# Moving weight splits one block ahead, a scaling behind the dealt work, and one product behind another, in an attention and two-layer expert kernel

## The chip, the cores and the metric

One Trainium2 chip, one of its cores. The metric is the device time of one execution in microseconds; the median of three runs of the kernel before is 670.41 us (670.06 to 671.7).

## What is computed

The reference chains three steps on 1152 tokens. Step 2 is where the change is.

```python
x = attention(q, k, v)                 # 8 heads, windowed or dilated, -> (1152, 512)
p = domain_probs / (domain_probs.sum(-1, keepdims=True) + 1e-09)
for e in range(4):                     # dense mixture: every token meets every expert
    h = np.maximum(x @ w1[e], 0.0)     # (1152, 512) @ (512, 1024)
    out += p[:, e:e + 1] * (h @ w2[e]) # (1152, 1024) @ (1024, 512)
h = out @ w_in                         # (1152, 512) @ (512, 2048)
g = P(h) / (Q(h) + 1e-6)               # a rational function, Q with |h|
return g @ w_out                       # (1152, 2048) @ (2048, 512)
```

## The kernel before

**Tiling.** Tokens lie in three chunks of 384 (c = 0, 1, 2), each of three tiles of 128 (t = 0 to 8). Hidden columns lie in units of 256 (u); two units are a group (g). Groups 0 to 7 are the four experts, groups 8 to 11 the last layer. Every fp32 operand is split into a high and a low part, and each product is made of three matmuls (high x high, high x low, low x high). The split of a weight is two steps: ScalarE casts the raw tile to its high part (line 777), VectorE subtracts it from the raw tile to get the low part (line 781), each in two halves of 128x512.

**A blocked group** (g = 2 to 7) has this order on TensorE (lines 994 to 1023). First `h_paced(u, 0)`, 24 matmuls of chunk 0 for the first unit (line 337); then the output tile 6 of the group before (`o_paced`, 12 matmuls, line 382); then `h_paced(u + 1, 0)` for the second unit; then output tiles 7 and 8. Behind these, `strassen(u, ...)` and `strassen(u + 1, ...)` make the hidden values of chunks 1 and 2 of one unit in seven products of six matmuls (line 886) in place of eight, with an output tile put between the products at three places (`then(0)`, `then(1)`, `then(2)`); the last tile of the second block is left out in group 7. In what follows a block is one call of `strassen`, a pair is two products in a row. In group 2 no output tile 6 stands ahead of the second unit.

**Inside a block.** The first product goes to `y`, and ScalarE copies it to `z` (line 900). Another product, the fifth, goes to `v`; ScalarE copies it to `p5` (line 904). The product that is third in the program, the sixth, is added up on `y`, and VectorE then adds `y` and `p5` into `v` (line 893). The next product on `y` has to wait for that sum, since it changes `y`.

**What sets the order.** A planner (`Pace`) deals the work of VectorE and ScalarE while it writes TensorE's program. `passed(us)` moves TensorE's planned clock on by the cost of a step (h 2.09 for half a chunk, o 2.74, p 1.045) and emits what VectorE can do by then. Two lists feed it. `later(wait, cost, key, f)` puts an item that is due at a set time. `behind(cost, key, f)` puts an item in a queue that is served in order; weight splits (`split_later`), sums of weight blocks (`sums_later`, line 797) and their casts (`sums_split_later`, lines 806 and 811) go there. What is left of VectorE's planned time is filled with pieces of the conversion of the last layer's float64 weights (`convert`, lines 140 to 182), whose result is stored through a single buffer `w` by SP's queue (line 145). `settle(key)` emits at once all that stands in the queue up to the named item; `h_paced(u, c)` settles the split of `w1[u]`.

**The output tile.** An output tile has one of two PSUM banks (`pso`). From group 1, tile 3 on until group 7, tile 0, ScalarE scales it by the expert's weight into `part` (line 412) and GpSimd adds `part` to the sum by a DMA (line 413). Elsewhere VectorE adds it (line 415).

**Raw weights.** They come by DMA into four buffers (line 84). The next three loads, `w1` of unit u + 3 and `w2` of units u + 2 and u + 3, are issued by SP once VectorE has made the low part of the sums of unit u + 1 (line 811).

Of the kernel before, what the change touches and what calls it, by code (L numbers as in the profile page):

```python
# [23 lines left out]
ALU = mybir.AluOpType  # L24
# [22 lines left out]
def body(ctx, tc, qkv, mask, dp, w1, w2, w1d, w2d, coef, out):  # L47
    nc = tc.nc
# [455 lines left out]
    with tc.manual_schedule():  # L504
# [353 lines left out]
        def o_paced(g, t):  # L858
            for v in range(2):
                settle(("h", 2 * g + v, t // 3))  # L860
                settle(("w2", 2 * g + v))
            ps = o_bank()
            for v in range(2):
                o_half(g, t, v, ps)
            if by_dma(g, t):
                o_sum(g, t, ps)
            passed(COST["o"])
            if not by_dma(g, t):
                later(0.2, COST["osum"], ("o", g, t), lambda: o_sum(g, t, ps))

        def strassen(u, between_):

            for k in (("w1", u), ("sw", u, 0), ("sw", u, 1), "tokens"):
                if k != ("sw", u, 0) or u % 2 == 0:
                    settle(k)
            yz, vz = h_tile(), h_tile()
            z, y, v, q = yz[:, 0, :TC], yz[:, 1, :TC], vz[:, 0, :TC], vz[:, 1, :TC]
            w = [i.rearrange("p (h k i f) -> p h i k f", h=2, k=2, i=2) for i in (w1s[u][:, 0], w1s[u][:, 1])]
            block = lambda m, h, i: [t[:, h, i] for t in m]
            x = lambda c, h: [t[:, 2 * h:2 * h + 2] for t in xt[c]]  # L880
            t_ = lambda n: [t[:, n] for t in tt]
            s = lambda h, i: [sw[u, i][:, n, h] for n in range(2)]
            def product(out, a, b, first=False):
                for k in range(2):
                    for n, (i, j) in enumerate(((0, 0), (0, 1), (1, 0))):
                        nc.tensor.matmul(  # L886
                            out, lhsT=a[i][:, k], rhs=b[j][:, k],
                            start=first and k + n == 0, stop=k + n == 3, skip_group_check=not first,
                        )
                passed(COST["p"])  # L890

            def add(out, a, b):
                later(0.2, COST["add"], ("add", u), lambda: nc.vector.tensor_tensor(out=out, in0=a, in1=b, op=ALU.add))

            def then(n):
                for f, *args in between_[n]:
                    f(*args)

            product(y, block(w, 0, 0), x(1, 0), first=True)
            nc.scalar.copy(z, y)  # L900
            then(0)
            product(v, s(1, 1), x(2, 0), first=True)
            p5 = st.tile([128, TC], F32, tag="p5", name="p5")
            nc.scalar.copy(p5, v)
            settle(("sw", u, 0))
            product(y, s(0, 0), t_(0))
            add(v, y, p5)
            then(1)
            settle(("add", u))
            product(y, s(0, 1), t_(1))  # L910
            add(q, y, p5)
            product(z, block(w, 1, 0), x(1, 1))
            then(2)
            settle(("add", u))
            product(v, s(1, 0), x(2, 1))
            product(y, block(w, 1, 1), t_(2))
            for c, ps, wait in ((1, yz, 1.1), (2, vz, 2.0)):
                high, low = relu_parts(u, c, ps)
                high()
                later(wait, COST["relu"], ("h", u, c), low)  # L920
# [42 lines left out]
        for g in range(NG):  # L963
            u = 2 * g
            more = g + 1 < NG
            again = g + 1 in BLOCKED
            o = lambda *at: [(o_paced, *i) for i in at]
            if g == 0:
                temp = token_sums()
                for v in range(2):  # L970
                    h_paced(v, 2)
                for j in range(3):
                    o_paced(0, 6 + j)
                continue
            if g == 1:
                loads((load_w2, u + 2), (load_w2, u + 3))
                split_later(w1s, "w1", u + 2)
                for n in range(3):
                    tokens_later(temp[n], *(t[:, n] for t in tt), wait=12.0)
                o_paced(1, 0)  # L980
                settle("tokens")
                t1 = first_sum()
                split_later(w2s, "w2", u + 2)
                split_later(w1s, "w1", u + 3)
                sums_later(u + 2)
                o_paced(1, 1)
                o_paced(1, 2)
                for v in range(2):
                    h_paced(u + v, 2)
                tokens_later(t1, *(t[:, :2] for t in xt[2]))  # L990
                sums_split_later(u + 2, 1)
                sums_split_later(u + 2, 0, [(loads, (load_w1, u + 4))])
                sums_later(u + 3)
                for j in range(3):
                    o_paced(1, 3 + j)
                continue
            if g in BLOCKED:
                h_paced(u, 0)
                sums_split_later(u + 1, 1)
                split_later(w2s, "w2", u + 1)  # L1000
                if again:
                    split_later(w1s, "w1", u + 2)
                if g > 2:
                    o_paced(g - 1, 6)
                h_paced(u + 1, 0)
                if g > 2:
                    o_paced(g - 1, 7)
                    o_paced(g - 1, 8)
                strassen(u, [o((g - 1, j if g > 2 else j + 3)) for j in (3, 4, 5)])
                sums_split_later(u + 1, 0, [(loads, (load_w1, u + 3), (load_w2, u + 2), (load_w2, u + 3))])  # L1010
                if again:
                    sums_later(u + 2)
                    sums_split_later(u + 2, 1)
                strassen(u + 1, (o((g, 0)), o((g, 1)), o((g, 2)) if again else []))
                if again:
                    sums_split_later(u + 2, 0, [(loads, (load_w1, u + 4))])
                    split_later(w2s, "w2", u + 2)
                    split_later(w1s, "w1", u + 3)
                    sums_later(u + 3)
                else:  # L1020
                    loads((load_w1, u + 4), (load_w1, u + 5))
                    o_paced(g, 2)
                    for j in range(3):
                        o_paced(g, 3 + j)
                        if j < 2:
                            settle(("o", g, 2))
                            x2_half(0, j)
                continue
            if g == NG1:
                while Pace.due:  # L1030
                    run_due(Pace.due.index(min(Pace.due)))
                st_pool.__exit__(None, None, None)
                Rational.pool = ctx.enter_context(tc.tile_pool(name="rat", bufs=3))
                o_tile(g - 1, 6)
                x2_half(1, 0)
                x2_half(1, 1)
                h_step(u, 0)
                h_step(u + 1, 0)
                between.clear()
                r1, r2 = pairs  # L1040
                r1.third()
                o_tile(g - 1, 7)
                r1.fourth()
                r1.fifth()
                o_tile(g - 1, 8)
                r2.denominator()
                r2.numerator()
            else:
                h_step(u, 0)
                h_step(u + 1, 0)  # L1050
                o_step(g - 1, 2)
            extra = {}
            if more:
                split_w1(u + 2)
                loads((load_w2, u + 2))
            h_step(u, 1)
            if g == NG1:
                x2_turn(2, 0)
                extra = {0: [(x2_turn, 2, 1), (x2_split, 2, 0), (x2_split, 2, 1)]}
            if more:  # L1060
                split_w1(u + 3)
                loads((load_w2, u + 3))
            h_step(u + 1, 1)
            if g == NG - 1:
                break
            o_step(g, 0, extra)
            if more:
                split_w2(u + 2)
            if g + 2 < NG:
                loads((load_w1, u + 4))  # L1070
            h_step(u, 2)
            if more:
                split_w2(u + 3)
            if g + 2 < NG:
                loads((load_w1, u + 5))
            h_step(u + 1, 2)
            o_step(g, 1)
# [150 lines left out]
```

## Time and profile before

| | |
|---|---|
| median of 3 runs | 670.41 us |
| the profiled execution | 670.22 us |
| its span, first to last instruction | 668.4 us |
| mean granted clock of TensorE | 0.988 of full speed |
| TensorE busy | 640.4 us, 96% of the span |
| VectorE busy | 501.6 us, 75% |
| ScalarE busy | 334.6 us, 50% |

The profiled execution lies 1.8 us over its span and 0.2 us under the median. TensorE is busy for nearly all of the span, and its busy time contains matmuls at half clock as well as at full clock. So what is to be had is read from two places: the time in which TensorE waits, and the stretches in which its granted clock is below full.

### The profile page before, as it was taken

Reading aid. Unit: us, or ns where it says so; the run is one execution under the profiler, and the core shown is the slowest. Engines: PE = TensorE matmul, PEld = TensorE weight load, DVE = VectorE, ACT = ScalarE, POOL = GpSimd, SP = SyncE. Lnnn points to the kernel's source line nnn. Section 1 sums busy time; section 2 is a strip of 40 time slices with the busy share of each in tenths; the row PEclk is TensorE's granted clock in tenths of the full one; section 3 lists DMA queues with packets and bytes.
Section 4 is the critical chain, followed back from the end, with each engine's and each line's share of the span. In section 5 each row is a group of like instructions: output and inputs, shape, how many; then the busy total and the mean of one; then the engine's idle time right before and its main releaser. Section 6 shows DMA issues by size and latency. Waiting matters only on the chain.

```text
span 668.4 us, 9664 instructions
## 1 busy us (share of the span) xinstructions
PE 640.4 (96%) x3766; PEld 567.6 (85%) x3767; DVE 501.6 (75%) x742; ACT 334.6 (50%) x621; POOL 83.0 (12%) x92
## 2 busy tenths in 40 slices
PE   8999999899989989989989989999999999999996
PEld 4888897798978878878978979889999999999985
DVE  6677249577766857876876874865899999999986
ACT  5986414244434444445444553324656555555551
POOL 2312080411102102111111111100000000000000
PEclk9999999999989989989999999999999999999999
DMA  9983024165936855864874883880330330300012
GB/s 283 256 232 117 1 64 151 71 151 135 264 111 158 255 139 141 238 204 102 249 199 112 256 239 76 241 336 1 126 119 9 126 126 1 126 0 1 1 48 94
DMA packets 33053, 92.92 MB, mean 139 GB/s; under 512 B 3536, under 2 KB 4048, under 8 KB 30960
## 3 DMA queue, kind: packets, MB, share of 16 engines
q1 hardware_dynamic: 25376, 78.77, 35.9%
q0 software_dynamic: 7344, 13.37, 11.5%
q8 instruction: 29, 0.48, 0.3%
q10 hardware_dynamic: 288, 0.16, 0.1%
q14 instruction: 16, 0.13, 0.1%
HBM read 59.79 MB, written 19.14 MB: 118 GB/s over the span
## 4 chain that ended last, share of the span: by engine, by line
PE 85%; DVE 8%; ACT 4%; issue 2%; DMA 1%; DVEq 0%; ACTq 0%
PE ps_o L382 39%; PE ps_h L337 29%; PE ps_h L886 12%; ACT pr L266 2%; PE ps_v L301 1%; PE ps_s L287 1%; DVE w L781 1%; DMA w<-w 1%; DVE hl L358 1%; DVE t L845 1%; PE ps_h L436 1%; PE ps_s L234 1%; DVE t L160 1%; ACT w L777 1%; PE ps_h L583 1%
## 5 line engine op out<-in xcount | busy, mean ns | idle before, releaser
L382 PE MATMUL ps_o<-w,hh 128*128 128x512 f32 x832 | 225.5, 393 | 2.1 <-DVE acc L415 2.1
L337 PE MATMUL ps_h<-xh,w 128*128 128x384 f32 x768 | 208.6, 345 | 13.6 <-ACT w L777 10.1
L382 PEld LDWEIGHTS ps_o<-w,hh 128*128 128x128 f32 x832 | 154.4, 188 | 32.4 <-DVE acc L415 2.8
L337 PEld LDWEIGHTS ps_h<-xh,w 128*128 128x128 f32 x768 | 142.8, 193 | 18.6 <-ACT w L777 12.2
L337 PE MATMUL ps_h<-xl,w 128*128 128x384 f32 x384 | 130.6, 340 | 0.0
L382 PE MATMUL ps_o<-w,hl 128*128 128x512 f32 x416 | 129.2, 392 | 0.9 <-DVE hl L358 0.9
L382 PEld LDWEIGHTS ps_o<-w,hl 128*128 128x128 f32 x416 | 77.8, 188 | 18.9 <-DVE hl L358 2.1
L412 ACT ACTIVATE part<-ps_o,p_sb 128x512 f32<-128x512 f32 x51 | 35.2, 690 | 105.1 <-PE ps_o L382 73.1
L358 DVE SCALAR_TENSOR_TENSOR hl<-ps_h,hh 128x768 fp32r<-128x768 f32 x48 | 44.7, 952 | 44.5 <-ACT hh L354 44.1
L413 POOL DMA_DIRECT2D acc<-part x51 | 44.5, 872 | 257.8 <-ACT part L412 241.9
L337 PEld LDWEIGHTS ps_h<-xl,w 128*128 128x128 f32 x384 | 74.1, 193 | 0.5
L354 ACT ACTIVATE hh<-ps_h 128x768 fp32r<-128x768 f32 x48 | 37.6, 809 | 58.1 <-PE ps_h L337 55.3
L474 ACT ACTIVATE ab<-sq,cbias 128x768 f32<-128x768 f32 x24 | 22.7, 944 | 37.2 <-DVE sq L470 36.9
L144 DVE TENSOR_TENSOR w<-f,w 128x512 fp32r<-128x512 f32 x32 | 22.0, 688 | 24.8 <-ACT w L140 24.7
L781 DVE TENSOR_TENSOR w<-raw,w 128x512 fp32r<-128x512 f32 x48 | 31.8, 685 | 8.5 <-ACT w L777 8.3
L465 ACT ACTIVATE sq<-ps_h 128x768 f32<-128x768 f32 x24 | 19.3, 803 | 32.3 <-PE ps_h L337 32.3
L140 ACT CAST w<-f 128x512 fp32r<-128x512 f32 x32 | 19.8, 619 | 26.7 <-DVE f L182 13.8
L266 ACT ACTIVATE pr<-pr,mx 128x80 f32<-128x80 f32 (+1 forms) x84 | 29.7, 357 | 6.6 <-DVE mx L259 6.5
L886 PE MATMUL ps_h<-xh,sw 128*128 128x384 f32 x96 | 29.1, 343 | 1.7 <-DVE hl L358 1.0
L886 PE MATMUL ps_h<-t,sw 128*128 128x384 f32 x144 | 29.6, 340 | 0.0
L886 PE MATMUL ps_h<-xh,w 128*128 128x384 f32 x96 | 28.3, 335 | 0.0
L777 ACT CAST w<-raw 128x512 fp32r<-128x512 f32 x48 | 28.1, 616 | 0.0
(94 smaller groups left out, 892.6 us busy)
## 6 DMA issues: line engine op xcount, KB each, us to landing
w<-w SPq DMA_DIRECT2D x32, 512.0 KB, 3.9
w<-w SPq DMA_DIRECT2D x16, 1024.0 KB, 6.8
raw<-in_w_dram SPq DMA_DIRECT2D x30, 512.0 KB, 6.4
acc<-part POOLq DMA_DIRECT2D x51, 256.0 KB, 4.2
x<-in_w1d_dram SPq DMA_DIRECT2D x16, 512.0 KB, 4.1
x<-in_w2d_dram SPq DMA_DIRECT2D x16, 512.0 KB, 3.7
out_dram<-acc SPq DMA_DIRECT2D x8, 256.0 KB, 2.2
v<-in_qkv_dram SPq DMA_DIRECT2D x6, 320.0 KB, 8.0
```

Of the source, the lines that this page charges most:

```text
L144: nc.vector.tensor_tensor(out=w[:, 1], in0=f, in1=w[:, 0].bitcast(F32), op=ALU.subtract)
L266: nc.scalar.activation(pr[:, j, i], pr[:, j, i], AF.Exp, scale=-1.0, bias=self.mx[:, j, i:i + 1], accum_out=self.total[:, j, i:i + 1],)
L337: nc.tensor.matmul(ps[:, i, :TC], lhsT=a[:, k, f], rhs=b[:, k], start=k + n == 0, stop=k + n == 5,)
L354: nc.scalar.activation(new_h(u, c)[0], ps[:, :, :TC], AF.Relu)
L358: nc.vector.scalar_tensor_tensor(out=hl, in0=ps[:, :, :TC], scalar=0.0, in1=hh.bitcast(F32), op0=ALU.max, op1=ALU.subtract,)
L382: nc.tensor.matmul(ps, lhsT=a[:, i, tk], rhs=b[:, i], start=v + n == 0, stop=v + n == 6)
L412: nc.scalar.activation(part, ps, AF.Copy, scale=pe)
L413: nc.gpsimd.dma_start(acc[t], part, accum_op=ALU.add)
L474: nc.scalar.activation(self.ab, self.sq, AF.Ln, bias=cbias)
L777: nc.scalar.copy(store[u][:, 0, s_], raws[nm, u][:, s_])
L781: nc.vector.tensor_tensor(out=w[:, 1, s_], in0=raws[nm, u][:, s_], in1=w[:, 0, s_].bitcast(F32), op=ALU.subtract)
L886: nc.tensor.matmul(out, lhsT=a[i][:, k], rhs=b[j][:, k], start=first and k + n == 0, stop=k + n == 3, skip_group_check=not first,)
```

## The change

Four edits, all in the groups of the experts.

- `o_paced`: the planner's time of the tile passes (and the work that is dealt for it is emitted) before ScalarE's scaling of the tile is emitted, not behind it.
- `strassen`: the sixth product goes ahead of the fifth. The sum of the two then follows ScalarE's copy of the fifth, and is due 0.8 us behind it, not 0.2 us behind the sixth.
- Blocked groups: the split of `w2[u + 2]` and `w1[u + 3]` is queued between the two blocks, not behind the second. The cast of the sums of unit u + 1, with the three loads that hang on it, is queued ahead of the last output tile of the first block, not behind the block.
- Group 1: the split of token sums is queued without its 12 us of delay, the split of `w1[u + 3]` follows it, and the second output tile goes ahead of the settling of the token sums.

```diff
@@ o_paced
             for v in range(2):
                 o_half(g, t, v, ps)
+            passed(COST["o"])
             if by_dma(g, t):
                 o_sum(g, t, ps)
-            passed(COST["o"])
-            if not by_dma(g, t):
+            else:
                 later(0.2, COST["osum"], ("o", g, t), lambda: o_sum(g, t, ps))
@@ strassen
             then(0)
+            settle(("sw", u, 0))
+            product(y, s(0, 0), t_(0))
             product(v, s(1, 1), x(2, 0), first=True)
             p5 = st.tile([128, TC], F32, tag="p5", name="p5")
             nc.scalar.copy(p5, v)
-            settle(("sw", u, 0))
-            product(y, s(0, 0), t_(0))
-            add(v, y, p5)
+            later(0.8, COST["add"], ("add", u), lambda: nc.vector.tensor_tensor(out=v, in0=y, in1=p5, op=ALU.add))
             then(1)
@@ group 1
                 for n in range(3):
-                    tokens_later(temp[n], *(t[:, n] for t in tt), wait=12.0)
+                    tokens_later(temp[n], *(t[:, n] for t in tt))
+                split_later(w1s, "w1", u + 3)
                 o_paced(1, 0)
+                o_paced(1, 1)
                 settle("tokens")
                 t1 = first_sum()
+                sums_later(u + 2)
                 split_later(w2s, "w2", u + 2)
-                split_later(w1s, "w1", u + 3)
-                sums_later(u + 2)
-                o_paced(1, 1)
                 o_paced(1, 2)
@@ blocked groups
-                strassen(u, [o((g - 1, j if g > 2 else j + 3)) for j in (3, 4, 5)])
-                sums_split_later(u + 1, 0, [(loads, (load_w1, u + 3), (load_w2, u + 2), (load_w2, u + 3))])
+                fills = [o((g - 1, j if g > 2 else j + 3)) for j in (3, 4, 5)]
+                free = [(loads, (load_w1, u + 3), (load_w2, u + 2), (load_w2, u + 3))]
+                fills[2].insert(0, (sums_split_later, u + 1, 0, free))
+                strassen(u, fills)
                 if again:
                     sums_later(u + 2)
                     sums_split_later(u + 2, 1)
+                    split_later(w2s, "w2", u + 2)
+                    split_later(w1s, "w1", u + 3)
                 strassen(u + 1, (o((g, 0)), o((g, 1)), o((g, 2)) if again else []))
                 if again:
                     sums_split_later(u + 2, 0, [(loads, (load_w1, u + 4))])
-                    split_later(w2s, "w2", u + 2)
-                    split_later(w1s, "w1", u + 3)
                     sums_later(u + 3)
```

The order of the instructions shows it at three places.

**Place 1: ScalarE at the start of group 4**, from the end of the block before to the relu (`hh`) of the second unit's chunk 0. `L777 CAST w1` is the high part of the second unit's weights, `L412` the scaling of output tile 6, `L140` and `L163` belong to the conversion. Before:

```order
L806 CAST sw_2479<-raw_2062 128x512
L777 CAST w2_2498<-raw_2358 128x512
L354 ACTIVATE hh_2500<-ps_h_2461 128x768
L412 ACTIVATE part_2516<-ps_o_2503,p_sb_82 128x512
L140 CAST w_2520<-f_2446 128x512
L163 ACTIVATE x64_2430<-x64_2430 128x512
L777 CAST w2_2498<-raw_2358 128x512
L777 CAST w1_2528<-raw_2356 128x512 x2
L354 ACTIVATE hh_2558<-ps_h_2533 128x768
```

and now, in the same stretch:

```order
L806 CAST sw_2500<-raw_2072 128x512
L354 ACTIVATE hh_2519<-ps_h_2485 128x768
L806 CAST sw_2540<-raw_2307 128x512
L412 ACTIVATE part_2542<-ps_o_2522,p_sb_82 128x512
L777 CAST w2_2564<-raw_2311 128x512
L140 CAST w_2578<-f_2470 128x512
L163 ACTIVATE x64_2426<-x64_2426 128x512
L777 CAST w2_2564<-raw_2311 128x512
L354 ACTIVATE hh_2587<-ps_h_2545 128x768
```

Both casts of the second unit's `w1` have left the stretch; they stood behind the scaling of tile 6 and ahead of the relu that ends it.

**Place 2: ScalarE in the block before that**, from the copy `z` (`L900`) to the end of the block; `L906` is the copy of the fifth product, `w1_2450` the weights that place 1 lost. Now:

```order
L900 COPY ps_h_2340<-ps_h_2340 128x384
L412 ACTIVATE part_2371<-ps_o_2355,p_sb_82 128x512
L806 CAST sw_2381<-raw_2072 128x512
L777 CAST w2_2394<-raw_2309 128x512
L906 COPY p5_2396<-ps_h_2341 128x384
L777 CAST w2_2394<-raw_2309 128x512
L412 ACTIVATE part_2415<-ps_o_2398,p_sb_82 128x512
L777 CAST w1_2450<-raw_2307 128x512
L140 CAST w_2453<-f_2385 128x512
L163 ACTIVATE x64_2324<-x64_2324 128x512
L777 CAST w1_2450<-raw_2307 128x512
L412 ACTIVATE part_2459<-ps_o_2436,p_sb_82 128x512
```

The first cast of `w2` for the next group now stands ahead of the copy of the fifth product, and it reads a tile whose load was issued in the block before.

**Place 3: VectorE in group 1**, around the low parts of the token sums (`L845`); `L415` adds an output tile and so frees its bank. Before:

```order
L409 TENSOR_SCALAR acc8_1473<-ps_o_1430,p_sb_82 128x512
L179 TENSOR_TENSOR f_1451<-f_1451,t_1428 128x512
L781 TENSOR_TENSOR w1_1471<-raw_849,w1_1471 128x512 x2
L845 TENSOR_TENSOR t1_1308<-ab_1306,t0_1307 128x768
L845 TENSOR_TENSOR t1_1308<-ab_1305,t0_1307 128x768
L845 TENSOR_TENSOR t1_1308<-ab_1304,t0_1307 128x768
L415 SCALAR_TENSOR_TENSOR acc0_864<-ps_o_1457,p_sb_82,acc0_864 128x512
```

and now:

```order
L409 TENSOR_SCALAR acc8_1473<-ps_o_1430,p_sb_82 128x512
L179 TENSOR_TENSOR f_1451<-f_1451,t_1428 128x512
L781 TENSOR_TENSOR w1_1471<-raw_849,w1_1471 128x512
L415 SCALAR_TENSOR_TENSOR acc0_864<-ps_o_1457,p_sb_82,acc0_864 128x512
L781 TENSOR_TENSOR w1_1471<-raw_849,w1_1471 128x512
L182 SCALAR_TENSOR_TENSOR f_1451<-x64_1350,f_1451 128x512
L845 TENSOR_TENSOR t1_1308<-ab_1306,t0_1307 128x768
```

The sum of group 1's first output tile has moved ahead of the three low parts.

## Rows read from the trace of the kernel before

**Rows 1.** The page: TensorE's granted clock in 40 slices, tenths of full speed.

```profile
PEclk9999999999989989989999999999999999999999
```

**Rows 2.** Waits of TensorE: total us, times, longest us.

```profile
PE ps_h L337 <- ACT w L777: 10.1, 5, 2.9
PE ps_o L382 <- DVE acc L415: 2.1, 1, 2.1
```

**Rows 3.** Timeline of ScalarE in group 4: start us, us.

```profile
241.56 0.69 ACT L412 ACTIVATE part<-ps_o,p_sb 128x512 f32<-128x512 f32 x1 [2.00 <-PE ps_o L382]
243.21 1.64 ACT L777 CAST w<-raw 128x512 fp32r<-128x512 f32 x3
```

**Rows 4.** Chain, five stalls: output tile 6, then tile 7 (start, us).

```profile
184.94 2.55 PE ps_o L382 x11
196.27 5.48 PE ps_o L382 x24
...
238.71 2.78 PE ps_o L382 x12
250.85 5.48 PE ps_o L382 x24
...
291.86 2.78 PE ps_o L382 x12
302.79 5.48 PE ps_o L382 x24
...
343.73 2.78 PE ps_o L382 x12
353.19 5.48 PE ps_o L382 x24
...
394.14 2.78 PE ps_o L382 x12
405.41 4.80 PE ps_o L382 x21
```

**Rows 5.** Chain, undisturbed: a pair, three products in a row, the same 24 matmuls.

```profile
260.16 2.10 PE ps_h L886 x12
269.89 3.14 PE ps_h L886 x18
287.70 4.16 PE ps_h L337 x24
```

**Rows 6.** Windows around the second and fourth stall: us, busy (x), PEclk, DMA, GB/s.

```profile
238.00:252.00 14.00, 10.90 (x47) 9.51 (x46) 6.16 (x11) 4.92 (x8) 0.89 (x1) 0.88 0.37 95
342.00:354.00 12.00, 10.00 (x51) 8.66 (x51) 6.69 (x10) 5.12 (x9) 0.86 (x1) 1.00 0.48 127
```

**Rows 7.** Chain, group 3's second block and group 7's end, where the tiles come late.

```profile
210.45 1.29 PE ps_h L886 x7
...
224.82 2.76 PE ps_o L382 x12
...
419.59 2.25 PE ps_h L886 x12
...
441.05 5.49 PE ps_o L382 x24
```

**Rows 8.** Timeline of ScalarE in group 3's second block.

```profile
221.37 0.62 ACT L140 CAST w<-f 128x512 fp32r<-128x512 f32 x1 [2.28 <-DMA w<-w]
222.97 0.48 ACT L900 COPY ps_h<-ps_h 128x384 f32<-128x384 f32 x1
```

**Rows 9.** The line of VectorE's sums in the blocks, ns min/median/max.

```profile
L893 DVE TENSOR_TENSOR ps_h<-ps_h,p x24: 555/566/567, 155.3 to 438.1; 128x384 f32<-128x384 f32 x24
```

**Rows 10.** The line of the raw loads, windows 220:232 and 324:336.

```profile
DMA to landing us min/median/max: 5.1/5.8/6.6
...
L84 SPq DMA_DIRECT2D raw<-in_w_dram x3: 328/616/1235, 324.4 to 328.1; - x3
DMA to landing us min/median/max: 6.5/7.5/8.2
```

## The prediction

> **What bounds the kernel now.** I read the page first: TensorE's granted clock is full except in a few slices [rows 1], so the question is where TensorE stands still and where the clock falls with it. The waits of TensorE come next. One cause holds most of them: five waits for ScalarE's cast of `w1`, 10.1 us together; a single wait of 2.1 us for a sum on VectorE is the next [rows 2].
>
> ScalarE's timeline shows why the cast is late. The settling of the second unit's weights puts the casts into ScalarE's program behind the scaling of output tile 6, and that scaling can only start when the tile is done, at 241.56. The casts follow from 243.21 on [rows 3]. But the end of tile 6 is just the moment at which TensorE wants the cast weights.
>
> The full price is more than the wait. The chain gives it as the time from the end of tile 6 to the start of tile 7, between which stand the second unit's 24 matmuls, 4.16 us when nothing disturbs them [rows 4, 5]:
>
> - 184.94 + 2.55 = 187.49 to 196.27: 8.78, lost 4.62
> - 241.49 to 250.85: 9.36, lost 5.20
> - 294.64 to 302.79: 8.15, lost 3.99
> - 346.51 to 353.19: 6.68, lost 2.52
> - 396.92 to 405.41: 8.49, lost 4.33
>
> Together 20.7 us. The part beyond the waits is the clock: around the second stall it is 0.88 on average over 14 us, so some 3.4 us at 1.2 GHz, half of which is lost; around the fourth, the shortest, it stays at 2.4 GHz [rows 6].
>
> **The change part by part.** The sum is made against the profiled execution, 670.2 us (span 668.4 and 1.8 around it), 0.2 under the median.
>
> *Splits one block ahead (with the scaling behind the dealt work).* The order shows both `w1` casts of the second unit in the block before (place 2), at two of its output tiles. One more block lies between them and their use: three tiles of 2.76 and seven products of about 1.05 are some 15 us, and the first unit's 24 matmuls and tile 6 come on top. So neither cast nor low part can be what TensorE waits for at the second unit. The moved work is four casts of ScalarE and four low parts of VectorE in each of five groups; no instruction is added. Inside the earlier block it lies beside TensorE's work: ScalarE is busy for half of the span. **-20.7 us**. The scaling's own move lets ScalarE use the time of a tile for the dealt casts instead of standing still until the tile is done; the two edits go together here.
>
> *Group 1.* The sum that frees the bank of the group's first tile now goes ahead of the three low parts of the token sums (place 3). The third tile needs that bank; it waited 2.1 us [rows 2]. **-2.1 us**. The second tile's sum is now behind the low parts, but its bank is wanted again only two h steps of 24 matmuls later, 8.3 us. Other work that the edit pulls forward (the split of `w1[u + 3]`) fills VectorE before its first use in group 2.
>
> *Fifth behind sixth, and what it gives the banks.* In the second block of group 3 the chain takes 14.37 us from 210.45 to the tile at 224.82 [rows 7]. A pair, a tile, three products, a tile and a pair are 2.10 + 2.76 + 3.14 + 2.76 + 2.10 = 12.86 [rows 5, 7], so 1.5 us are lost. There ScalarE held the relu and the copy behind a cast of the conversion that waited 2.28 us for the store of the single buffer [rows 8], and the fifth product, which starts on a PSUM tile, had to wait for that tile to come free. With the fifth behind the sixth it asks for the tile one product, 1.05 us, later. From 419.59 to 441.05, at the end of group 7, 21.46 us stand against three tiles, four pairs and three products in a row, 8.28 + 8.40 + 3.14 = 19.82, so 1.6 us. This stretch had conversion pieces in it; in the new order the last of them stand in group 7's first block. **-3.1 us**, both together, of which I would not be surprised to see a third stay.
>
> *What the swap takes.* The copy `z` had a product, a tile and nothing else to hide behind before the sixth product; it had the fifth in addition, and loses it: 2.76 us instead of 3.81. The sum of the two products had a tile less its own 0.56 us [rows 9] as slack; now the copy `p5` (as long as that of `z`, 0.48 us [rows 8]) comes first, so 1.7 us are left. I bound what may come of this from both sides. Below: nothing, if ScalarE is punctual. Above: two of twelve blocks as late as the copy at 222.97, 4.5 us behind the undisturbed end of its product at 218.45 [rows 8], so 4.5 + 0.5 - 2.76 = 2.2 us each. I take 0.7 us for all blocks, nearer to nothing, since the row's cause (a cast ahead of the copy that waits for a store) stands in the new order at two second blocks only, with some 7 us between the stores there.
>
> *Loads one block closer to their use.* In four groups the first `w2` cast now stands ahead of the copy `p5` (place 2). Count from the end of the product behind the second tile in the block before (line 910), which is the last to read the buffer that the sums of the next unit go to. ScalarE casts the sums, VectorE makes the low part behind about four of its own items: an estimate of 3.1 us from casts of about 0.55 [rows 3] and sums of 0.56 [rows 9]. SP then issues `w1`, and `w2` up to 1.2 us later; a load of these trios lands 5.1 to 8.2 us behind its issue [rows 10]. That is 8.2 to 12.5. Up to the cast, TensorE makes four products and two tiles, 4.2 + 5.5 = 9.7, and ScalarE a scaling and a cast, so it is there at about 11.0. The product that wants the sum of this block comes behind two more products and a tile: 6 x 1.05 + 3 x 2.76 = 14.6. The cast, the copy and the sum take some 1.7 us. So a load may land at 12.9 before TensorE notices, 0.4 us behind the slowest one. Bounds: 0, and 2 us in each of four groups if landing is as much later as the trios vary (3.1 us). I take 0.7 us in all. [...]
>
> Sum: 20.7 + 2.1 + 3.1 = 25.9 off, 1.4 on: 670.2 - 24.5 = **645.7 us**.
>
> **The rivals.**
>
> *The loads come late (B).* With the new casts of `w2` ahead of the copy `p5`, ScalarE waits for DMA and TensorE with it. For it: the margin is 0.4 us, and VectorE, with the same work in 25 us less, may run behind. Against: the first landings of the trios are well inside. Four waits of 2 us give 645.7 + 8 = 654; if they pull the clock down as the second stall did, four of 4.5, some 663.
>
> *The conversion holds ScalarE (C).* Its casts, dealt during a tile, wait for the store of the single buffer and now stand ahead of a scaling or a copy. Two or three waits of 2.2 us: about 651.
>
> *Every block waits for `z` (D), the slower side.* ScalarE's copy stands behind the scaling, which itself stands behind the dealt casts, and the sixth product asks for it 1.05 us sooner. If that were as late in every block as in [rows 8], twelve waits of 2.2 us eat 26 us: 671, and with the clock's fall, some 2 us each by the stalls above, about 695. It decides from 2.1 us per block on. Against: the dealt casts now run during the tile, so the scaling's queue gets shorter, not longer.
>
> *Nothing moves (E).* The second unit's wait stays because something else ends it then (the raw load). Against: its load is issued a whole block earlier than its cast. About 669.
>
> **How the numbers follow.** My forecast, new waits of 0 to 3.5 us, has 0.74: 644 to 648. B 0.12, C 0.09, D 0.03, E 0.02. The range takes in the forecast, C, and B's lower half, and below it half a microsecond more of small waits that may go: 643.5 to 652.5. A measurement of this kernel can tell about 0.3%, 2.0 us, from no change; faster by more than that has 0.95, same 0.02, slower 0.03.
>
> **What would show it.** In the profile of the changed kernel the row of TensorE waiting for the cast of `w1` is gone; tile 6 to tile 7 takes 4.2 us in every group; the granted clock has no slice below full between 100 and 440 us; group 1's third tile follows the second at once. A wait of TensorE for the copy or the sum in the blocks, or of ScalarE's cast on a raw load, would show B or C, and in all twelve blocks D. I am wrong if the five stalls stay, or if waits inside the blocks sum to over 5 us.

## The result, and the profile after

The changed kernel takes 646.22 us (median of 4 runs, 645.87 to 646.3) against 670.23 of the kernel before beside it: a ratio of 0.964, 95% interval 0.962 to 0.966. The forecast was 645.7. Its profiled execution took 646.3 us.

The page of the profiled execution: its span, the busy engines, TensorE's granted clock in 40 slices, and the engines' shares of the chain of waits.

```profile
span 644.5 us, 9658 instructions
...
PE 630.6 (98%) x3767; PEld 562.4 (87%) x3767; DVE 502.0 (78%) x742; ACT 334.7 (52%) x621; POOL 83.0 (13%) x92
...
PEclk9999999999999999999999999999999999999999
...
PE 92%; DVE 5%; ACT 2%; issue 0%; DVEq 0%; ACTq 0%
```

TensorE is busy for 630.6 us in place of 640.4, with the same matmuls: what is less is the time of matmuls that ran at half clock in the slices of [rows 1]. VectorE and ScalarE do the work that they did before. The waits of TensorE (total, times, longest):

```profile
PE ps_h L337 <- DVE hl L358: 2.0, 1, 2.0
...
PE ps_o L382 <- DVE hl L358: 0.9, 1, 0.9
PE ps_h L886 <- DVE ps_h L893: 0.7, 1, 0.7
```

Both rows of [rows 2] are gone. The 2.0 lies in the attention at 35 us and the 0.9 in front of group 1, at 107; the 0.7 is the only one of this table in the blocked groups. The chain (start us, us) has, in order of time, group 1's tiles, the five places of [rows 4] (the first with tile 6, the second unit's 24 matmuls, and tiles 7 and 8; of the others the 24 matmuls), and the two places in the blocks where something is left:

```profile
107.63 14.37 PE ps_o L382 x62
122.00 8.35 PE ps_h L337 x48
...
182.33 2.76 PE ps_o L382 x12
185.09 4.18 PE ps_h L337 x24
189.28 5.48 PE ps_o L382 x24
...
232.99 4.18 PE ps_h L337 x24
...
251.34 0.04 issue
251.39 2.38 PE ps_h L886 x12
...
281.19 4.18 PE ps_h L337 x24
...
329.08 4.18 PE ps_h L337 x24
...
376.98 4.18 PE ps_h L337 x24
...
395.34 2.10 PE ps_h L886 x12
...
410.98 2.12 PE ps_h L886 x12
...
413.12 0.57 DVE ps_h L893
...
413.74 2.37 PE ps_h L886 x12
416.12 5.49 PE ps_o L382 x24
```

The second unit takes 4.18 us in every group (4.16 in [rows 5]). The two places left are a pair that starts late in group 4's first block (2.38 + 0.04 for 2.10, 0.3 us), and the end of group 7, where two pairs take 416.12 - 410.98 = 5.14 in place of 4.20. The late pair in the timelines of ScalarE and VectorE: the conversion's cast waits for the store of its buffer, and the copy `p5` and the sum stand behind it.

```profile
249.17 0.62 ACT L140 CAST w<-f 128x512 fp32r<-128x512 f32 x1 [1.91 <-DMA w<-w]
...
250.77 0.57 DVE L907 TENSOR_TENSOR ps_h<-ps_h,p 128x384 f32<-128x384 f32 x1 [0.25 <-ACT p L906]
```

The tiles at the end of group 7 begin at 416.12, in [rows 7] at 441.05: 24.93 us earlier. Piece by piece: the five stretches of [rows 4] give 41.46 - 5 x 4.18 = 20.6; group 1's tiles end at 122.00, in the chain of before at 124.38, 2.4; group 3's stretch of [rows 7] takes 12.88, 1.5; the end of group 7 gives 0.7 (20.78 from 395.34 to 416.12, where [rows 7] have 21.46); group 4's late pair takes 0.3. Together 24.9.

At the last output tiles it is still 24.97 (613.26, before 638.23), but the spans differ by 23.9 only. From the end of VectorE's last sum to the end of the span, where the profile shows no engine at work any more, the changed kernel takes 5.1 us (639.42 to 644.5) and the kernel before 4.0 (664.42 to 668.4). Of the twelve traces below, two (`after_again`, `minus_scaling`) have 5.1 as well and ten have 4.0 to 4.2. Taking back the splits, the swap, the early loads or group 1's order by itself ends it, so it is no one edit's price. So where kernels differ by about 1 us, the medians are set beside a stretch of the traces that does not contain this end: from the start of group 1's tiles to the start of the last output tiles, 107.63 to 613.26, 505.6 us in the changed kernel.

### The profile page after: what moved, and what is told of

It is laid out like the page before. It is cut to its first block, busy times and chain, and to the rows that moved or that the text cites. A ratio compares the mean times of both kernels' runs of the same rounds, so it can differ in the third digit from the quotient of the medians.

```text
span 644.5 us, 9658 instructions
## 1 busy us (share of the span) xinstructions
PE 630.6 (98%) x3767; PEld 562.4 (87%) x3767; DVE 502.0 (78%) x742; ACT 334.7 (52%) x621; POOL 83.0 (13%) x92
## 4 chain that ended last, share of the span: by engine, by line
PE 92%; DVE 5%; ACT 2%; issue 0%; DVEq 0%; ACTq 0%
PE ps_o L382 43%; PE ps_h L337 30%; PE ps_h L886 14%; PE ps_v L301 2%; PE ps_s L287 1%; PE ps_s L234 1%; ACT pr L266 1%; PE ps_h L436 1%; PE ps_h L583 1%; PE ps_h L382 0%; DVE t L160 0%; DVE hl L358 0%; ACT pt L291 0%; DVE u L480 0%; DVE acc L421 0%
## 5 line engine op out<-in xcount | busy, mean ns | idle before, releaser
L337 PE MATMUL ps_h<-xh,w 128*128 128x384 f32 x768 | 202.9, 337 | 2.0 <-DVE hl L358 2.0
L337 PEld LDWEIGHTS ps_h<-xh,w 128*128 128x128 f32 x768 | 139.3, 188 | 3.4 <-DVE hl L358 2.2
L337 PE MATMUL ps_h<-xl,w 128*128 128x384 f32 x384 | 128.5, 335 | 0.0
L337 PEld LDWEIGHTS ps_h<-xl,w 128*128 128x128 f32 x384 | 72.1, 188 | 0.7
L412 ACT ACTIVATE part<-ps_o,p_sb 128x512 f32<-128x512 f32 x51 | 35.1, 688 | 68.3 <-PE ps_o L382 43.4
L358 DVE SCALAR_TENSOR_TENSOR hl<-ps_h,hh 128x768 fp32r<-128x768 f32 x48 | 44.7, 952 | 27.8 <-ACT hh L354 27.6
L140 ACT CAST w<-f 128x512 fp32r<-128x512 f32 x32 | 19.8, 618 | 20.1 <-DMA w<-w 11.2
L777 ACT CAST w<-raw 128x512 fp32r<-128x512 f32 x48 | 28.5, 615 | 1.1 <-DMA raw<-in_w_dram 1.1
L163 ACT ACTIVATE x<-x 128x512 f32<-128x512 f32 x32 | 21.7, 679 | 13.3 <-DVE t L160 13.2
```

The source lines that it names most:

```text
L337: nc.tensor.matmul(ps[:, i, :TC], lhsT=a[:, k, f], rhs=b[:, k], start=k + n == 0, stop=k + n == 5,)
L358: nc.vector.scalar_tensor_tensor(out=hl, in0=ps[:, :, :TC], scalar=0.0, in1=hh.bitcast(F32), op0=ALU.max, op1=ALU.subtract,)
L412: nc.scalar.activation(part, ps, AF.Copy, scale=pe)
L777: nc.scalar.copy(store[u][:, 0, s_], raws[nm, u][:, s_])
```

## The experiments

Twelve runs were made, ten kernels and two repeats, in three comparisons of four, each beside the kernel before: 671.43, 670.71 and 670.49 us. What was to be told apart is which edit carries the gain. My theory was the forecast's: the splits' place is the gain, the scaling only goes with it, the swap of fifth and sixth cures the late blocks. The rival was that ScalarE's scaling is the point, since all that stands behind it waits for a tile.

### One edit alone

`only_scaling` is the kernel before with the first edit:

```diff
+            passed(COST["o"])
             if by_dma(g, t):
                 o_sum(g, t, ps)
-            passed(COST["o"])
-            if not by_dma(g, t):
+            else:
```

> The kernel before with one edit: ScalarE's scaling of an output tile behind the work dealt for that time. My theory (the casts of the second unit's w1 are emitted by the settling at the second unit, behind tile 6 as a whole): the five stalls stay, shorter by the one or two casts that now precede the scaling; 1 to 4 us faster than before, 666 to 669 us, TensorE still waits five times for the cast of w1, over 7 us in total. Rival (the scaling's place is what held the casts): the stalls go, 650 to 653 us.

664.58 us (664.23 to 666.58), ratio 0.9913, interval 0.9881 to 0.9946. It gives more than mine said and far less than the rival's. Its waits of TensorE, and two of the five stalls as windows (us, busy and count of PE, PEld, DVE, ACT, POOL, then PEclk, DMA share, GB/s):

```profile
PE ps_h L337 <- ACT w L777: 9.1, 5, 1.9
```

```profile
236.00:250.00 14.00, 12.01 (x58) 10.13 (x58) 7.61 (x14) 5.95 (x10) 0.89 (x1) 1.00 0.30 85
288.00:302.00 14.00, 11.96 (x51) 10.24 (x50) 6.37 (x12) 4.12 (x7) 0.87 (x1) 0.88 0.33 95
```

The five stalls stay, but the longest is 1.9 us, not 2.9, and at three of them the clock holds at 2.4 GHz. From tile 6 to tile 7 it is 6.7, 6.7, 8.2, 6.7 and 8.2 us: 15.6 lost, not 20.7. The shorter waits and the clock are 5.1 us of gain. Three more places differ: group 3's stretch of [rows 7] is undisturbed (12.88), the end of group 7 takes 20.78 in place of 21.46, and group 1's tiles take 1.6 more, with the clock down. Together that makes 5.7 us; the spans (668.4 and 662.8) differ by 5.6. What the scaling leaves standing are the five waits.

`only_splits` is the kernel before with the edit of the blocked groups alone (the fourth hunk of the change).

> The kernel before with one edit: the blocked groups' queue (splits between the two blocks, sums and loads ahead of the first block's last tile). My theory: this alone takes the five stalls, 20.7 us, whatever the scaling's place: 648 to 651 us, no wait of TensorE for the cast of w1, the 2.1 us of group 1 and some of the late banks stay. Rival (the dealt casts now stand behind scalings in the blocks, ScalarE comes late to the copies, so both edits are needed): 655 to 662 us with waits of TensorE for ScalarE's copies or VectorE's sums inside the blocks.

653.83 us (653.64 to 653.93), ratio 0.9746, interval 0.9712 to 0.978: between the two. The waits of TensorE:

```profile
PE ps_h L886 <- DVE ps_h L893: 2.5, 4, 0.8
...
PE ps_h L886 <- DVE hl L358: 1.0, 4, 0.3
```

The five stalls are gone, but new short waits for VectorE stand in the blocks, and group 1's wait of 2.1 us stays.

### One edit taken back

In `minus_splits` both splits of `w2[u + 2]` and `w1[u + 3]` are queued behind the second block again; the rest is the changed kernel.

```diff
-                    split_later(w2s, "w2", u + 2)
-                    split_later(w1s, "w1", u + 3)
                 strassen(u + 1, (o((g, 0)), o((g, 1)), o((g, 2)) if again else []))
                 if again:
                     sums_split_later(u + 2, 0, [(loads, (load_w1, u + 4))])
+                    split_later(w2s, "w2", u + 2)
+                    split_later(w1s, "w1", u + 3)
```

> The changed kernel with the split of w2[u + 2] and w1[u + 3] queued behind the second block again; scaling, swap, loads and group 1 stay as changed. If the splits' place is what took the five stalls: they come back as in the run with the scaling's edit alone (TensorE waits five times for the cast of w1, 9 to 10 us, and loses 14 to 17 us in all), 660 to 663 us. If the scaling's place took most of them: 650 us or less.

666.35 us (665.27 to 668.29), ratio 0.9935, interval 0.9915 to 0.9956. The five waits are back as in `only_scaling`, and the end of group 7 is worse than in any other kernel here:

```profile
PE ps_h L337 <- ACT w L777: 9.1, 5, 1.9
PE ps_h L886 <- DVE ps_h L893: 3.8, 1, 3.8
```

So the place of the splits is worth 20 us within the change. In this trace it is 8.3, 8.0, 6.7, 8.2 and 6.7 us from tile 6 to tile 7, so 17.1 lost, with the clock down at three places; another 4.7 are lost at the end of group 7, where it is 23.40 us from the first block's last tile to the tiles at the end, and 18.68 in the changed kernel. Together 21.8; the profiled execution took 667.69 us, 21.4 more than that of the changed kernel. In the chain, with the DMA of the conversion's single buffer in it (415.13 and 438.53 begin and end the 23.40):

```profile
415.13 2.42 PE ps_o L382 x11
...
423.74 8.25 DMA w<-w
...
434.62 3.91 PE ps_h L886 x12
438.53 5.46 PE ps_o L382 x24
```

The last pair takes 3.91 us in place of 2.1: the granted clock is down as well, 0.83 on average from 430 to 440 us.

`minus_scaling` is the changed kernel without the first edit.

```diff
-            passed(COST["o"])
             if by_dma(g, t):
                 o_sum(g, t, ps)
-            else:
+            passed(COST["o"])
+            if not by_dma(g, t):
```

> The changed kernel with the scaling ahead of the dealt work again. My theory: the scaling's place only uses slack of ScalarE: 646 to 648 us, within 1.5 us of the changed kernel. Rival (the two edits work together): 650 to 658 us, with waits inside the blocks.

652.84 us (651.69 to 653.25), ratio 0.9729, interval 0.9699 to 0.976. My theory fell here: within the change the scaling's edit carries 6.6 us (6.1 in the stretch from group 1's tiles to the last output tiles), although no stall at the second unit came back. TensorE waits inside the blocks:

```profile
PE ps_h L886 <- DVE ps_h L907: 4.0, 4, 1.5
```

(Line 907 is the first sum, `y` and `p5`; L893 is the others.) Group 3's first block shows how. Timelines of this kernel: ScalarE, VectorE, TensorE (start us, us, what, idle before and what ended it).

```profile
195.00 0.69 ACT L412 ACTIVATE part<-ps_o,p_sb 128x512 f32<-128x512 f32 x1 [2.03 <-PE ps_o L382]
195.58 0.61 ACT L777 CAST w<-raw 128x512 fp32r<-128x512 f32 x1
...
197.69 0.48 ACT L900 COPY ps_h<-ps_h 128x384 f32<-128x384 f32 x1
...
196.74 0.69 DVE L144 TENSOR_TENSOR w<-f,w 128x512 fp32r<-128x512 f32 x1 [4.02 <-ACT w L140]
...
204.53 0.56 DVE L907 TENSOR_TENSOR ps_h<-ps_h,p 128x384 f32<-128x384 f32 x1
...
205.14 1.33 PE L886 MATMUL ps_h<-t,sw 128*128 128x384 f32 x6 [1.54 <-DVE ps_h L907]
```

and the same stretch of the changed kernel:

```profile
192.71 0.61 ACT L777 CAST w<-raw 128x512 fp32r<-128x512 f32 x1
...
194.84 0.69 ACT L412 ACTIVATE part<-ps_o,p_sb 128x512 f32<-128x512 f32 x1
195.86 0.46 ACT L900 COPY ps_h<-ps_h 128x384 f32<-128x384 f32 x1 [0.32 <-PE ps_h L886]
...
193.87 0.69 DVE L144 TENSOR_TENSOR w<-f,w 128x512 fp32r<-128x512 f32 x1 [1.55 <-ACT w L140]
...
202.42 0.56 DVE L907 TENSOR_TENSOR ps_h<-ps_h,p 128x384 f32<-128x384 f32 x1
...
203.29 1.23 PE L886 MATMUL ps_h<-t,sw 128*128 128x384 f32 x6
```

With the scaling ahead, ScalarE stands still until the tile is done at 195, and the weight cast follows 2.9 us later than in the changed kernel. Behind it stands a cast of the conversion (L140). VectorE, which makes the low parts of these casts in its own order, stands still for that one for 4.02 us (1.55 in the changed kernel) and comes 2.1 us later to the sum, and TensorE stands still for the sum, 1.5 us. Group 5 has the same picture. In groups 4 and 6 TensorE waits 0.45 us, and there the sum also waits for the copy `p5`, which stands behind a conversion cast that waits for the store of its buffer.

Between 160 and 430 us VectorE waits for the weight casts 16.8 us (first row: this kernel) and 1.7 us in the changed kernel (second row); with the casts of the sums and of the conversion it is 43.8 against 19.8. ScalarE waits for output tiles 72.0 (third row) against 39.9 us, with nearly the same busy time in that window, 128.8 and 128.4:

```profile
DVE w L781 <- ACT w L777: 16.8, 9, 3.0
...
DVE w L781 <- ACT w L777: 1.7, 3, 1.1
...
ACT part L412 <- PE ps_o L382: 72.0, 35, 5.0
```

`minus_swap` is the changed kernel with the fifth product ahead of the sixth and the sum due 0.2 us behind the sixth, as before.

```diff
-            settle(("sw", u, 0))
-            product(y, s(0, 0), t_(0))
             product(v, s(1, 1), x(2, 0), first=True)
...
+            settle(("sw", u, 0))
+            product(y, s(0, 0), t_(0))
+            add(v, y, p5)
             then(1)
```

> The changed kernel with the fifth product ahead of the sixth again. My theory: the swap gives the fifth product's PSUM tile 1.05 us more, worth 0 to 2 us where the relu before it is late: 646 to 648.5 us. Rival (the swap's cost, the later copy of the fifth product ahead of the sum, shows): 645.5 us or less, without the 0.3 us that TensorE now loses behind the second tile in group 4's first block.

644.98 us (644.52 to 645.77), ratio 0.9616, interval 0.9587 to 0.9645. The late block of group 3 does not come back: its chain has nothing but pairs and tiles of the usual length. So the swap is not needed for it; `only_scaling`, with the old order of the products, has it undisturbed too. A second comparison, below, asks for the swap's price.

`late_loads` puts the cast of the sums and the loads that hang on it behind the first block again; the splits stay early.

```diff
-                fills[2].insert(0, (sums_split_later, u + 1, 0, free))
                 strassen(u, fills)
+                sums_split_later(u + 1, 0, free)
```

> The changed kernel with the cast of the sums of unit u + 1, and the three raw loads that hang on it, queued behind the first block again, 4 to 5 us later. If the loads were as near to being late as the prediction put it (0.4 us to spare for the slowest): ScalarE waits in four groups some 2 to 4 us for a raw load with the scalings and copies queued behind it, TensorE waits inside the second blocks, 650 to 660 us. Rival (the queue moves the casts back with the loads, so that the margin stays): within 1.5 us of the changed kernel, 646 to 647.5 us, and ScalarE's wait for raw loads under 4 us in total.

646.86 us (646.43 to 646.88), ratio 0.964, interval 0.9619 to 0.9661: no difference in the median. Yet ScalarE now waits for raw weights (the line of the cast, what its idle time ended with), 10.8 us where the changed kernel has 1.1:

```profile
DMA raw<-in_w_dram: 10.8, 5
```

TensorE's pieces in the chain have their usual length at all five of these waits. It waits once elsewhere, 1.0 us, for the low part of the sums, which this edit puts later as well: at group 3's second block, with small delays in groups 4 and 6. From group 1's tiles to the last output tiles this kernel takes 507.2 us, 1.6 more than the changed one; its shorter end (4.1 for 5.1) hides 1.0 of that in the median. So the margin of the loads, which the forecast counted to 0.4 us, is wider than that.

`minus_group1` puts back group 1's order.

```diff
-                    tokens_later(temp[n], *(t[:, n] for t in tt))
-                split_later(w1s, "w1", u + 3)
+                    tokens_later(temp[n], *(t[:, n] for t in tt), wait=12.0)
                 o_paced(1, 0)
-                o_paced(1, 1)
                 settle("tokens")
                 t1 = first_sum()
-                sums_later(u + 2)
                 split_later(w2s, "w2", u + 2)
+                split_later(w1s, "w1", u + 3)
+                sums_later(u + 2)
+                o_paced(1, 1)
                 o_paced(1, 2)
```

> The changed kernel with group 1 as before. If its price is the 2.1 us wait alone: 648.3 us. If the clock falls behind that wait, as the runs with one edit showed in the window from 120 to 130 us (0.83 of full), another 1.7 us: 650 us.

647.59 us (647.09 to 649.88), ratio 0.9665, interval 0.9643 to 0.9687: 1.4 us by the medians, with one wait of 2.1 for the row L415 as in [rows 2] and the clock full around it. The stretch to the last output tiles takes 508.1 us, 2.4 more than in the changed kernel; the end is 1.0 shorter here.

### The swap's price, and where the scaling's gain sits

`minus_swap_again` repeats `minus_swap`, on one chip with the changed kernel itself (`after_again`).

> The changed kernel as it is, beside the three runs that follow, since it was not timed on the chip of the earlier ones. 646.2 us, and 644.5 of span.

> The fifth product ahead of the sixth again, once more, to tell 1 us from nothing. Theory (the swap has a price: the copy hides behind less, and group 4's first block waits 0.3 us): 1.0 to 1.4 us under the changed kernel of this same comparison, about 645.0. Rival (the earlier 645.0 was the other chip's): within 0.4 us of it.

647.01 us (646.25 to 647.76), ratio 0.9657, and 645.71 (644.65 to 649.1), ratio 0.9646 with an interval of 0.9618 to 0.9673. The medians again differ by 1.3 us, but the runs overlap, so this comparison alone decides nothing. The traces settle it. The stretch from group 1's tiles to the last output tiles takes 505.63 us in both traces of the changed kernel and 505.36 and 505.34 in the two without the swap: 0.3 us, the late pair in group 4. The other 1.0 is the end behind VectorE's last sum (5.1 and 4.0 to 4.1); four kernels with the swap have 4.1 or less too, so it is not the swap's price.

`minus_scaling_swap` takes back both the first edit and the swap.

> The scaling ahead of the dealt work again and the fifth ahead of the sixth again: splits and group 1 alone. Theory (the scaling costs by itself, whatever the order of the two products): 652 to 653.5, which is the blocked groups' queue alone, 653.8, less the 1.4 us of group 1. Rival (the scaling costs only because the swap put the copy p5 and the sum so close before their use): 649 or less.

650.98 us (650.36 to 651.49), ratio 0.9717, interval 0.969 to 0.9744: between the two, nearer to the theory. Without the swap the scaling is worth 650.98 - 645.71 = 5.3 us, with it 5.8 to 6.6 (652.84 against the changed kernel's 647.01 and 646.22); in the stretch of the traces it is 5.7 and 6.1. TensorE's waits are now for other items of VectorE:

```profile
PE ps_h L886 <- DVE hl L358: 2.9, 4, 1.3
...
PE ps_h L886 <- DVE ps_h L893: 1.8, 3, 0.7
```

`scaling_back_sum_now` is `minus_scaling` with the first sum emitted right behind the copy `p5`:

```diff
-            later(0.8, COST["add"], ("add", u), lambda: nc.vector.tensor_tensor(out=v, in0=y, in1=p5, op=ALU.add))
+            nc.vector.tensor_tensor(out=v, in0=y, in1=p5, op=ALU.add)
+            Pace.dv += COST["add"]
```

> The scaling ahead of the dealt work again, but the sum of y and p5 put into VectorE's program right behind the copy p5, ahead of what the planner deals in the 0.8 us that follow. Theory (the scaling holds ScalarE, the casts behind it make VectorE's queue late, and TensorE waits since the sum stands in that queue): the waits of TensorE for this sum, 4.0 us with the sum dealt, fall to 1 us or less, and 647 to 649.5 us. Rival (the copy p5 itself is late, or what is late is something else of ScalarE's, so the sum's place changes nothing): 651.5 to 654, waits as they were.

652.86 us (650.0 to 654.29), ratio 0.9741, interval 0.9712 to 0.9769: nothing gained by the median. In the stretch of the traces it still takes 5.1 us more than the changed kernel, where `minus_scaling` takes 6.1; the theory asked for at least 3 us back. This version of it, that only the sum's place in VectorE's queue is late, fell. Waits of TensorE, then of VectorE from 160 to 430 us:

```profile
PE ps_h L886 <- DVE ps_h L907: 3.0, 5, 0.9
```

```profile
DVE ps_h L907 <- ACT p L906: 15.3, 5, 9.5
```

The waits for the sum get shorter but one more comes, and VectorE now stands still for the copy 15.3 us, where the changed kernel has 3.2. With the swap TensorE's waits are for L907, without it for `hl` and L893. What the three kernels with the scaling ahead have in common is that VectorE stands still longer for ScalarE's casts (of weights, sums and conversion together: 43.8, 45.4 and here 31.1 us, against 19.8 in the changed kernel) and TensorE then waits for VectorE. That the first makes the second is read from the traces; no run changed VectorE's order of the casts alone.

### A faster version

`best` drops the swap and treats the two waits that were left: group 7's output tile 1 is dealt in two halves, at the second and third place of the last block (the third was empty), and VectorE's planned time is put 2.5 us further ahead of group 0, so that fewer conversion pieces stand ahead of the low part that group 1 waits for.

```diff
                 temp = token_sums()
+                Pace.dv += 2.5
...
-                strassen(u + 1, (o((g, 0)), o((g, 1)), o((g, 2)) if again else []))
+                strassen(u + 1, (o((g, 0)), o((g, 1)) if again else [(o_split, g, 1, 0)], o((g, 2)) if again else [(o_split, g, 1, 1)]))
```

> The changed kernel without the swap of the fifth and sixth product, and with two further edits: the output tile 1 of the last group is cut in two halves, one at the second and one at the third place of the last block (against TensorE's wait of 0.7 us for VectorE's second sum there), and the conversion is dealt 2.5 us later from group 0 on (against the wait of 0.9 us for a low part of group 0's second unit). If both waits go and none comes: 1.5 us under the run without the swap, 643.5 us. Rival (the later dealing moves the conversion into the blocks and makes new waits there): 645 us or more.

643.11 us (642.68 to 643.13), ratio 0.9585, interval 0.9564 to 0.9605. From 90 to 445 us one wait of TensorE is left; the stretch with the end of group 7 is 49.73 busy of 50 at full clock:

```profile
390.00:440.00 50.00, 49.73 (x258) 44.33 (x257) 21.02 (x28) 15.10 (x22) 2.50 (x3) 1.00 0.44 142
```

It is the fastest of the kernels here, some 3 us under the changed one, of which 1.0 is the shorter end. Which of its three edits gives how much was not run apart; against `minus_swap` the trace has group 1's hidden values begin 1.4 us earlier (120.57 for 121.94), though their start varies by as much between the two traces of the changed kernel (122.00 and 123.47), and it gains 0.5 from there to the end of group 7, less than the 0.9 of the wait there, since one new wait of 0.3 us came.

## Why the prediction was right, and where its steps were not

**The total and the signs.** 645.7 was forecast, 646.2 measured. So near a hit is in part luck: the swap and the loads took 0.3 where 1.4 stood, the banks gave 2.2 where 3.1 stood, group 1 gave 0.3 more, and the 1.1 us behind the last sum had no term. All four signs came: no row of the cast, 4.18 us in each group, no slice of the clock below full, group 1's tiles in one piece of 14.37 us.

**The five stalls, 20.7.** In the trace it went, as counted (20.6). That the splits' place ends the waits is shown from both sides: `only_splits` and `minus_scaling` have none of them, `only_scaling` and `minus_splits` all five. But the two edits' shares overlap: the scaling alone takes 5.1 us off the same stalls.

**"The two edits go together here."** This is the step that fell short. That the scaling's move spares ScalarE the standstill was right, but the forecast gave it no term of its own. Without it the change loses 5.3 to 6.6 us, in a place that the forecast did not price: inside the blocks, by way of VectorE. The splits one block ahead put four more casts and four more low parts there; with ScalarE standing still for each tile, these casts come too late for VectorE's order. I had said the moved work "lies beside TensorE's work", by ScalarE's busy half; but ScalarE's busy time is the same with and without this edit, and what differs is when the casts come.

**"Fifth behind sixth, and what it gives the banks", 3.1.** Of the 3.1, group 3's 1.5 came whole and 0.7 of group 7's 1.6; 0.9 stayed, about the third that the text allowed for. But it is not the swap that brought it: `minus_swap` keeps the gain, and `only_scaling` alone has both pieces. The mechanism of the forecast is not refuted by that. At this place in group 3 the fifth product waits for its PSUM tile (the row `hl` L358) in the three kernels that have neither the scaling's edit nor the swap: 0.80 us before, 0.34 in `only_splits`, 1.29 in `minus_scaling_swap`. With either edit the wait is gone, with the swap alone too (`minus_scaling`, where TensorE comes 1.5 us later to the place). Beside the scaling's edit the swap has nothing left to give. What stayed in group 7 the chain explains: the last block has no third tile, so its last two products come right behind the pair before them, and wait for that pair's sum (413.12).

**Swap and loads, 1.4 on.** The swap costs 0.3 us (forecast 0.7), by the conversion's cast that waits for its buffer, as rival C had it, though in a first block where the forecast had named two second ones. The loads cost nothing that the trace shows, although they landed 4.6 to 9.0 us behind their issue between 160 and 400 us, where the forecast had counted 8.2 as the slowest. It was the cover that was larger: in `late_loads` ScalarE waits 10.8 us for loads, and TensorE's work at these five places is undisturbed.

**Group 1, 2.1.** The trace shows 2.4 gained, and 2.4 lost again in the stretch of `minus_group1`; the 1.4 of the medians contains the 1.0 by which its end is shorter.

**The rivals.** D and E are out by the trace. B's and C's conditions exist (ScalarE waits for loads, once, and for the single buffer), and cost 0.3 us in one block. The step that fell short is nearly as large as the room that the range left above the forecast: without the scaling's edit, 652.8 would have lain just above its end of 652.5.

What stays open: what decides whether 4.0 or 5.1 us stand behind VectorE's last sum, and why the end of group 7 gets so much worse in `minus_splits`; that the conversion is less far along there is argued from the chain, not tried.

## What to carry to other kernels

On an engine whose instructions follow one another in program order, as ScalarE's do in these timelines, put an instruction that must wait for TensorE's result behind whatever is ready by then, not ahead of it: the standstill is not only that instruction's, it can go on to an engine that is fed from behind it, as to VectorE here. When two edits seem to "go together", price each without the other; here the one without a term held 5.3 to 6.6 of 24 us. Putting the one item that is waited for first in its queue need not help when what the queue is fed with is late: here it gave back 1.0 of 6.1 us. And before a difference of 1 us between two kernels is called an edit's, compare a stretch of the traces that holds the edit.

## What the runs showed that I had not expected

Waits of about 2 us do not always bring the clock down from 2.4 to 1.2 GHz. The 2.1 us wait in group 1 stands in a window from 120 to 130 us with a granted clock of 1.00 in the kernel before and in `minus_group1`, and of 0.83 in `only_scaling` and `only_splits`; the five nearly equal waits of 1.9 us and less in `only_scaling` leave it full at three places and bring it to 0.88 over 14 us at two. What decides between them no run here tells.

```profile
120.00:130.00 10.00, 9.26 (x49) 8.72 (x50) 3.83 (x7) 1.98 (x4) 3.57 (x2) 1.00 0.16 52
```

```profile
120.00:130.00 10.00, 8.69 (x37) 7.75 (x38) 3.27 (x5) 0.00 (x0) 4.09 (x2) 0.83 0.14 42
```

(The first is `minus_group1`, the second `only_scaling`.) In `only_scaling` the same wait of 1.9 us thus costs 2.5 us where the clock holds and 4.0 where it falls; which of the two comes was not to be told ahead.
